# Batch 1 loaded in head halves, h of batches 0 and 1 summed in two steps, and a new order

## The chip, the cores and the metric

The kernel runs on one core of one Trainium2 chip. The metric is device time in microseconds; the time before is 179.36 us, the median of three runs (179.36 to 179.39). A core has engines that run side by side, each through its own list of instructions in order: PE (matrix products, with weight loads shown as PEld), DVE and ACT (elementwise work), POOL and SP (here they mostly issue transfers).

## The reference

```python
kv = einsum('bhsd,bhse->bhde', k, v)            # 8 batches, 8 heads, 576 rows, 64 columns
out = einsum('bhsd,bhde->bhse', q, kv)
x = out / sqrt(mean(out * out, -1) + 1e-6) * g_norm   # heads side by side: 576 x 512
h = maximum(x @ w_in, 0)                        # 512 -> 1024
conv = depthwise convolution of h along the rows, 3 taps, conv_w
y = (h * sigmoid(conv)) @ w_out                 # 1024 -> 512
```

Inputs and outputs are float32; the kernel calculates in bfloat16 with float32 sums.

## The kernel before

Everything is held transposed: columns of x and h lie on the 128 partitions, rows of the sequence along them. Two heads fill 128 partitions, so x of a batch has four blocks (head pairs) t, and h has eight blocks f. A pair of blocks is called u (u = 0 holds t 0 and 1, u = 1 holds t 2 and 3). The 576 rows are cut in two parts s, of 256 and 320 rows for batch 0, 288 and 288 for most others.

A batch goes through these steps, each a small function named by two letters:

- load of q, k and v (`Lq`, `Lk`, `Lv`: transfers on POOL's queue that also turn float32 into bfloat16). Batch 0 comes another way: as float32 by SP's and ACT's queues into staging tiles `stq` and `stg`, then cast on DVE (`cad`) or ACT (`caa`). `gt` makes POOL wait for one of these transfers (k 1) before it issues the weights: `Li` is half of w_in, `Lo` is w_out.
- `kv` (L398) and its copy to SBUF on ACT (`kva`) or DVE (`kvd`); `qt` transposes q (L429), copied by `qa` or `qd`.
- `ot` (L456): q times kv. `sq` (ACT, L505): squares. `on` (PE, L524): sums of squares over a head. `nl` (ACT, L541): reciprocal root, called rs. `mo` (DVE, L552): x. For batches 4 to 7, `oc`, `ss`, `ln`, `sl`, `sp` and `mu` do this for two batches together, and batches 6 and 7 have q transposed by a transfer on SP's queue (`tq`) and use a second copy of kv (`kx`, tile kvx, read by `ox` of s = 1).
- h: `hp` (L643, batch 0), `hs` (L624, batches 1 to 3, 6 and 7) or `hm` (L609, batches 4 and 5) multiply w_in by x: four matmuls, one for each t, are summed in one PSUM bank. `rp` (L650), `rh` (L636) or `re` (L615) apply the Relu on ACT.
- convolution and gate: on DVE in steps `ta`, `aa`, `ab`, with a sigmoid on ACT (`sg`, L683), then the product `mg` (L707); four blocks of batch 0 have the convolution on PE instead (`cv`, L693, with matrices that `dg` builds, and `sc`, L700).
- output: `om` multiplies by w_out (L717) for 128 rows of a pair of batches, `ea` (ACT, L723) or `ed` (DVE, L728) copies the row block, and `st` stores it on SP's queue.
- `fi` multiplies zeros (L282): matmuls whose result nobody uses.

The order is one long string, `ORDER`: tokens like `hp.1.0@0` (f 1, s 0, in PSUM bank 0). The loop at the end of the function calls the steps in that order, and then ties each instruction to the one before it on its engine, so each engine's list is exactly the string's order for that engine. Waits between engines follow from the data and from the buffers, which the number after @ picks. PSUM has eight banks; a bank is free for its next user when its last reader is done. Transfers from POOL carry eight completion counters in turn, and each waits for the one eight before it.

The first tokens of batch 0's h before, and the load of batch 1:

```
mo.0.0.1 fi.1.512@4 on.0.1.1@4 nl.0.1.1@3 mo.0.1.1 Li.0.4 hp.1.0@0 hp.3.0@1 hp.2.0@4 hp.0.0@5 rp.3.0@0 rp.2.0 rp.0.0
pc dg.2 hp.2.1@1 hp.0.1@4 rp.0.1 rp.1.0 hp.1.1@5 Li.4.4 rp.1.1 hp.3.1@2 hp.6.0@0 dg.0 cv.0.0@6 sc.0.0@0 rp.2.1 rp.6.0
```

`Li` and the loads stand here because nothing before them needs them in the string; POOL issues them as soon as its own list gets there.

Of the kernel before, what the change touches and what calls it, by code (L numbers as in the profile page):

```python
# [74 lines left out]
hs.1.5.1@4 ta.1.1.1 aa.1.1.0 ab.1.1.0 hs.1.5.0@5 rh.1.5.0 hs.1.4.1@7 rh.1.4.1 hs.1.4.0@0 rh.1.4.0 rh.1.5.1 hs.1.2.0@1
rh.1.2.0 hs.1.3.0@3 rh.1.3.0 kv.2.0.2@6 sg.0.1.5 mg.0.1.2 ta.1.1.2@1 om.0.3.0.4@3 kva.2.0.2@2 ot.2.1.1@4 ot.2.0.1@0
qt.3.0.0@6 qd.3.0.0@1 om.0.3.4.4 ed.0.3@0 Lk.3.0.4@1 Lv.3.0.4@1 Lq.4.0.4@1 Lk.4.0.4@0 Lv.4.0.4@0 sg.1.1.0 sg.1.1.1
ta.1.1.3 aa.1.1.1 om.0.0.4.4 sq.2.0.1@0 on.2.0.1@6 nl.2.0.1@8 mo.2.0.1@2 sq.2.1.1@1 om.0.1.0.4@3 om.0.1.4.4 ea.0.0@1
on.2.1.1@6 nl.2.1.1@9 mo.2.1.1 ot.2.1.0@0 sq.2.1.0@2 om.0.2.0.4@2 om.0.2.4.4 ed.0.2@2 ea.0.1@3 st.0.0 st.0.1
on.2.1.0@6 nl.2.1.0@0 mo.2.1.0 kv.3.0.2@4 kva.3.0.2@0 ot.2.0.0@2 sq.2.0.0@3 hs.2.0.1@6 mg.1.1.0 rh.2.0.1@1 hs.2.7.1@7  # L80
rh.2.7.1 ta.1.1.5@0 on.2.0.0@4 nl.2.0.0@1 mo.2.0.0 hs.2.3.1@6 rh.2.3.1 hs.1.7.1@7 rh.1.7.1 hs.1.7.0@0 rh.1.7.0
qt.4.1.0@4 qd.4.1.0@2 ot.3.0.1@6 sq.3.0.1@4 qt.3.1.0@2 qd.3.1.0@3 hs.2.3.0@0 rh.2.3.0 ab.1.1.1 on.3.0.1@4 nl.3.0.1@2
mo.3.0.1@0 hs.2.4.1@1 rh.2.4.1 ta.1.1.4 ot.3.1.1@2 sq.3.1.1@5 hs.1.6.0@0 rh.1.6.0 hs.2.4.0@4 rh.2.4.0 ot.3.0.0@6
sq.3.0.0@6 hs.2.2.0@1 rh.2.2.0 on.3.1.1@4 nl.3.1.1@3 hs.2.1.1@0 rh.2.1.1 hs.2.1.0@1 rh.2.1.0 aa.1.1.2 ab.1.1.2
mo.3.1.1 on.3.0.0@4 nl.3.0.0@4 mo.3.0.0 hs.2.2.1@0 rh.2.2.1 ot.3.1.0@2 sq.3.1.0@7 hs.3.1.1@1 rh.3.1.1 hs.3.2.1@0
rh.3.2.1 pl on.3.1.0@4 nl.3.1.0@5 mo.3.1.0 sg.1.1.2 hs.3.3.1@6 Lq.5.0.4@2 Lq.6.0.4@0 Lk.5.0.4@1 hs.3.7.1@7 hs.3.6.1@0
sg.1.1.3 qt.4.0.0@4 qd.4.0.0@0 rh.3.3.1 qt.5.0.0@2 qd.5.0.0@4 hs.3.5.0@1 rh.3.5.0 rh.3.6.1 rh.3.7.1 hs.3.5.1@4
rh.3.5.1 hs.2.0.0@5 hs.3.2.0@2 rh.2.0.0 sg.1.1.5 Lv.5.0.4@1 Lq.7.0.4@1 mg.1.1.1 ta.1.1.6@1 ta.1.1.7 aa.1.1.3
hs.3.0.1@1 rh.3.0.1 hs.3.3.0@0 kv.4.0.2@6 kvd.4.0.2@1 ab.1.1.3 sg.1.1.4 mg.1.1.2 rh.3.3.0 qt.5.1.0@4 qd.5.1.0@1
ta.2.2.3@0 rh.3.2.0 hs.2.6.1@3 rh.2.6.1 sg.1.1.7 sg.1.1.6 mg.1.1.3 hs.3.1.0@1 hs.2.7.0@6 rh.3.1.0 om.0.8.0.4@0  # L90
ot.4.0.0@2 sq.4.0.0@0 rh.2.7.0 ot.4.0.1@4 oc.4.0.1@6 sq.4.0.1@1 om.0.7.0.4@7 hs.3.0.0@1 rh.3.0.0 ta.2.2.2 ta.2.2.1@1
ta.2.2.0 om.0.8.4.4 ea.0.8@4 oc.4.0.0@7 om.0.7.4.4 ed.0.7@5 tq.7.1@3 st.0.7 ot.4.1.0@4 sq.4.1.0@2 oc.4.1.0@8
kv.5.0.2@0 ot.4.1.1@2 oc.4.1.1@9 om.0.4.0.4@6 sq.4.1.1@3 kvd.5.0.2@2 ot.5.0.1@0 aa.2.2.0 aa.2.2.1 ot.5.1.1@4
sq.5.1.1@4 sq.5.0.1@5 oc.5.1.1@0 tq.6.0@0 ab.2.2.0 om.0.4.4.4 ed.0.4@1 oc.5.0.1@1 om.0.5.0.4@7 ot.5.0.0@2 sq.5.0.0@6
ot.5.1.0@4 om.0.5.4.4 Lk.6.0.4@0 Lv.6.0.4@0 ed.0.5@3 hs.3.4.1@0 ab.2.2.1 sq.5.1.0@7 ss.4.4.2@1 ss.5.4.2 ln.4@0 sl.4@0
oc.5.1.0@2 hs.3.7.0@6 rh.3.7.0 om.0.6.0.4@7 rh.3.4.1 oc.5.0.0@3 hs.2.5.0@1 rh.2.5.0 hs.3.6.0@6 rh.3.6.0 kz.6.0.2@4
tq.6.1@2 kvd.6.0.2@0 kx.6@0 sp.4.1.0.4@2 mu.4.1.0@1 sp.4.0.0.4@0 mu.4.0.0 om.0.6.4.4 sg.2.2.1 sp.4.0.1.4@4 mu.4.0.1
sp.4.1.1.4@2 mu.4.1.1 hs.2.5.1@6 rh.2.5.1 ea.0.6@5 st.0.6 hs.3.4.0@0 rh.3.4.0 hs.2.6.0@1 rh.2.6.0 sp.5.0.1.4@4
mu.5.0.1@0 sp.5.1.0.4@6 mu.5.1.0 sg.2.2.0 mg.2.2.0 hm.4.7@2 re.4.7@0 hm.4.5@0 re.4.5 sg.2.2.3 sp.5.1.1.4@4 mu.5.1.1
# [35 lines left out]
def kernel(  # L135
# [511 lines left out]
    @op  # L647
    def rp(f, s):
        r0, r1 = RS[s]
        nc.scalar.activation(  # L650
            h_of(0, f).rearrange("p (e n r) -> p e n r", e=2, r=R)[:, :, :, r0:r1],
            T["hp", f, s].rearrange("p (e r n) -> p e n r", e=2, r=r1 - r0), AX.Relu)
# [157 lines left out]
```

## Time and profile before

| | |
|---|---|
| median of three runs | 179.36 us |
| profiled execution | 179.97 us, of which the span is 178.2 us |
| PE busy | 169.2 us (95%) |
| ACT busy | 150.5 us (84%) |
| DVE busy | 148.4 us (83%) |
| PE fillers (L282) | 40 recorded, 12.7 us |
| transfers of POOL's queue | 14.50 MB |

The span is what the profiler saw between the first and the last instruction; the execution's own time lies 1.77 us above it. Busy time is a union: matmuls overlap one another, so 320 matmuls of 286 ns each can have 43.5 us of busy time. The chain of waits follows the work back from the last instruction to what released it. A row of a timeline gives the start, the busy time, the engine, the line, the tiles and in brackets the idle time in front of it and what ended that.

### The profile page before, as it was taken

What the parts mean: (1) busy time and instruction counts of PE and PEld (TensorE: products, weight loads), DVE (VectorE), ACT (ScalarE), POOL (GpSimd) and SP (SyncE); (2) the same over time, 40 slices, a digit from 0 to 9 for tenths busy, and PEclk for the clock granted to TensorE, in tenths of its full rate; (3) what the DMA queues carried; (4) which work ended last, traced back from release to release, by engine and by line L of the source; (5) the groups of instructions that cost most, each with busy time, mean ns of one, the idle gap of its engine ahead of it and who ended that gap; (6) DMA issues with size and microseconds to landing.
All of it is one profiled execution on the core that took longest, in us unless ns stands there. A gap on an engine that the chain in (4) does not pass through costs nothing.

```text
span 178.2 us, 5048 instructions
## 1 busy us (share of the span) xinstructions
PE 169.2 (95%) x2093; PEld 101.1 (57%) x2109; DVE 148.4 (83%) x285; ACT 150.5 (84%) x273; POOL 20.5 (11%) x32
## 2 busy tenths in 40 slices
...
GB/s 163 392 316 207 208 207 207 209 208 207 207 213 253 208 209 206 181 167 144 174 151 159 135 4 15 180 0 161 109 146 0 0 0 59 123 97 81 318 316 190
DMA packets 25862, 29.10 MB, mean 163 GB/s; under 512 B 5988, under 2 KB 20336, under 8 KB 25840
## 3 DMA queue, kind: packets, MB, share of 16 engines
q0 software_dynamic: 13248, 14.50, 49.0%
...
q8 instruction: 16, 0.26, 0.6%
...
## 4 chain that ended last, share of the span: by engine, by line
PE 78%; ACT 15%; issue 3%; DVE 2%; ACTq 0%
PE banks L717 30%; PE banks L624 15%; PE banks L609 9%; PE banks L282 5%; ACT h L636 4%; PE banks L643 4%; ACT taps L683 3%; ACT sq L505 3%; PE banks L429 2%; PE banks L456 2%; PE banks L398 2%; PE banks L524 2%; PE banks L693 2%; ACT L223 1%; ACT rs L541 1%
## 5 line engine op out<-in xcount | busy, mean ns | idle before, releaser
L717 PE MATMUL banks<-w_out_sb,h 128*128 128x512 bf16 x268 | 63.4, 380 | 0.8 <-issue 0.3
L624 PE MATMUL banks<-x,w_in_sb 128*128 128x288 bf16 (+2 forms) x320 | 43.5, 286 | 1.0 <-issue 0.6
L683 ACT ACTIVATE taps<-taps,cw 128x576 bf16<-128x576 bf16 (+1 forms) x44 | 40.9, 971 | 3.8 <-DVE taps L677 3.8
L717 PEld LDWEIGHTS <-h 128*128 128x128 bf16 x280 | 26.2, 98 | 30.3 <-issue 1.3
L624 PEld LDWEIGHTS <-w_in_sb 128*128 128x128 bf16 x320 | 30.4, 98 | 11.3 <-issue 2.0
L636 ACT ACTIVATE h<-banks 128x288 bf16<-128x288 f32 (+2 forms) x80 | 30.3, 484 | 0.4 <-PE banks L624 0.2
L707 DVE TENSOR_TENSOR h<-h,taps 128x1152 bf16<-128x1152 bf16 (+1 forms) x24 | 22.9, 954 | 6.7 <-ACT h L650 4.1
L505 ACT ACTIVATE sq<-banks 128x576 bf16<-128x576 f32 (+2 forms) x32 | 20.9, 682 | 1.3 <-PE banks L456 1.2
L677 DVE TENSOR_TENSOR taps<-taps,h 128x1152 bf16<-128x1152 bf16 (+1 forms) x22 | 21.4, 973 | 0.5
L672 DVE TENSOR_TENSOR taps<-taps 128x1152 bf16<-128x1152 bf16 (+1 forms) x22 | 21.3, 978 | 0.5
L723 ACT ACTIVATE row<-banks 128x512 f32<-128x512 f32 x25 | 14.8, 603 | 6.0 <-PE banks L717 6.0
L666 DVE TENSOR_SCALAR taps<-h,cw 128x576 bf16<-128x576 bf16 (+1 forms) x44 | 18.5, 421 | 0.3 <-ACT h L650 0.2
L667 DVE TENSOR_SCALAR taps<-h,cw 128x576 bf16<-128x576 bf16 (+1 forms) x44 | 18.5, 421 | 0.0
L552 DVE SCALAR_TENSOR_TENSOR x<-banks,cw,rs 128x576 bf16<-128x576 f32 (+2 forms) x16 | 12.9, 816 | 5.4 <-ACT rs L541 5.3
L609 PE MATMUL banks<-x,w_in_sb 128*128 128x288 bf16 x128 | 16.7, 286 | 0.1
L609 PEld LDWEIGHTS <-w_in_sb 128*128 128x128 bf16 x128 | 12.3, 98 | 4.1 <-issue 0.5
L223 ACT ACT_TABLE_LOAD x10 | 12.8, 1283 | 2.0 <-issue 1.8
L282 PE MATMUL banks<-zero 128*128 128x512 bf16 x40 | 12.7, 450 | 1.4 <-DVE zero L261 1.2
L595 DVE SCALAR_TENSOR_TENSOR x<-o,cw,banks 128x576 bf16<-128x576 f32 (+2 forms) x16 | 12.1, 808 | 0.5 <-PE banks L589 0.5
L541 ACT ACTIVATE rs<-banks,eps_sb 128x576 f32<-128x576 f32 (+2 forms) x16 | 11.6, 738 | 1.1 <-PE banks L524 1.0
L517 ACT ACTIVATE o<-banks 128x576 f32<-128x576 f32 (+2 forms) x16 | 10.5, 683 | 0.5 <-PE banks L496 0.5
L615 ACT ACTIVATE h<-banks 128x576 bf16<-128x576 f32 x16 | 10.0, 673 | 0.5 <-PE banks L609 0.5
...
## 6 DMA issues: line engine op xcount, KB each, us to landing
...
q_sb<-in_q_dram POOLq DMA_DIRECT2D x7, 576.0 KB, 16.4
k_sb<-in_k_dram POOLq DMA_DIRECT2D x7, 576.0 KB, 13.0
v_sb<-in_v_dram POOLq DMA_DIRECT2D x7, 576.0 KB, 15.2
stg<-in_v_dram ACTq DMA_DIRECT2D x2, 576.0 KB, 6.2
...
```

Source lines behind the costliest of these rows:

```text
L282: nc.tensor.matmul(ps[:, :w], zero[:, :P], zero[:, :w], start=True, stop=True)
L505: nc.scalar.activation(T["sq", b, u, s], T["o", b, u, s], AX.Square)
L609: nc.tensor.matmul(ps[:, s, :HS], w_in_sb[:, t, f * P:(f + 1) * P], T["x", b][:, t, c0:c1], start=(t == 0), stop=(t == NT - 1))
L624: nc.tensor.matmul(ps, w_in_sb[:, t, f * P:(f + 1) * P], T["x", b][:, t, c0:c1], start=(t == 0), stop=(t == NT - 1))
L636: nc.scalar.activation(h, fr, AX.Relu)
L666: nc.vector.tensor_scalar_mul(tap[:, 0, f % 2, :n, 8:8 + S], h[:, f], cw[:, f:f + 1])
L667: nc.vector.tensor_scalar_mul(tap[:, 1, f % 2, :n, :S], h[:, f], cw[:, 2 * NF + f:2 * NF + f + 1])
L672: nc.vector.tensor_add(tap[:, 1, :, :n, :S], tap[:, 0, :, :n, 7:7 + S], tap[:, 1, :, :n, 1:1 + S])
L677: nc.vector.tensor_add(y, y, span(b, n)[:, 2 * j:2 * j + 2])
L683: nc.scalar.activation(y, y, AX.Sigmoid, scale=cw[:, NF + f:NF + f + 1])
L707: nc.vector.tensor_mul(h, h, tap_of(b, j)[:, 1, :, :n, :S])
L717: nc.tensor.matmul(T["om", p, m], h[:, f, m * P:(m + 1) * P], w_out_sb[:, f, :], start=(f == 0), stop=(f == NF - 1))
```

## The change

Batch 1's q, k and v, three transfers of four blocks each, become six of two blocks (head pairs u = 0 and u = 1). k and v of u = 0 are issued between the two halves of w_in, the others behind them. A new step `hk` does half of an h group: the matmuls of head pair u alone; its second call closes the sum in the same bank. It takes the place of `hp` (batch 0) and of `hs` for batch 1. All of `ORDER` is new, with other choices of engine for some copies: five casts of batch 0 on ACT in place of two, `kva` five in place of six, `qa` one in place of two, `ea` 23 in place of 25 (with DVE's counterparts the other way), one `oq` (the sum of squares in four small matmuls) in place of one `on`, 39 fillers in place of 44.

```diff
 ORDER = """
-pre@0,1 fi.10.512@0 caa.q.0.0@0 af pn ps cad.v.0.0@0 qt.0.0.0@2 qa.0.0.0@0 fi.8.512@0 ct@0 fi.6.512@1 gt.k.1.0
-caa.v.1.0 cad.k.0.0@0 cad.k.1.0 kv.0.0.1@4 fi.2.512@1 cad.v.2.0 cad.q.1.0 cad.v.3.0 cad.k.2.0 pg cad.k.3.0 cad.q.0.1
...
-qt.0.1.1@0 qd.0.1.1 ot.0.0.1@2 sq.0.0.1@2 ot.0.1.1@6 fi.1.512@0 sq.0.1.1@3 on.0.0.1@0 nl.0.0.1@2 mo.0.1.0 fi.1.512@4
-mo.0.0.1 fi.1.512@4 on.0.1.1@4 nl.0.1.1@3 mo.0.1.1 Li.0.4 hp.1.0@0 hp.3.0@1 hp.2.0@4 hp.0.0@5 rp.3.0@0 rp.2.0 rp.0.0
-pc dg.2 hp.2.1@1 hp.0.1@4 rp.0.1 rp.1.0 hp.1.1@5 Li.4.4 rp.1.1 hp.3.1@2 hp.6.0@0 dg.0 cv.0.0@6 sc.0.0@0 rp.2.1 rp.6.0
-dg.1 cv.0.1@4 sc.0.1 mg.0.1.0 dg.3 hp.4.1@3 rp.4.1 hp.4.0@6 rp.4.0 rp.3.1 hp.5.1@7 rp.5.1 hp.5.0@0 Lq.1.0.4@1
-Lk.1.0.4@1 Lv.1.0.4@1 rp.5.0 hp.7.1@1 rp.7.1 hp.6.1@6 rp.6.1 ta.0.1.5@1 ta.0.1.4 aa.0.1.2 cv.0.2@4 sc.0.2@0 cv.0.3@2
-sc.0.3 qt.1.0.0@0 qd.1.0.0@2 qt.1.1.0@6 qd.1.1.0@3 kv.1.0.1@4 kva.1.0.1@1 kv.1.1.1@2 ot.1.0.1@0 kva.1.1.1 sq.1.0.1@4
-mg.0.1.1 hp.7.0@4 rp.7.0 Lo.0.8 ta.0.1.7@0 ab.0.1.2 ot.1.1.1@2 sq.1.1.1@5 ta.0.1.6 on.1.0.1@6 nl.1.0.1@4 mo.1.0.1@1
-fi.6.512@5 fi.1.512@4 on.1.1.1@4 nl.1.1.1@5 mo.1.1.1 ot.1.0.0@6 sq.1.0.0@6 ot.1.1.0@4 sq.1.1.0@7 on.1.0.0@0 nl.1.0.0@6
-mo.1.0.0 hs.1.3.1@2 rh.1.3.1 aa.0.1.3 ab.0.1.3 hs.1.1.1@3 on.1.1.0@0 rh.1.1.1 nl.1.1.0@7 mo.1.1.0 hs.1.0.1@2 rh.1.0.1
...
+pre@0,1 af pn ps caa.q.0.0@0 cad.v.0.0@0 cad.k.0.0@0 fi.10.512@0 caa.v.3.0 cad.v.1.0 qt.0.0.0@2 fi.10.512@0 qd.0.0.0@0
+ct@0 fi.4.512@1 cad.k.1.0 kv.0.0.1@4 kva.0.0.1@0 cad.v.2.0 fi.4.512@1 caa.q.1.0 pg pc cad.k.3.0 caa.k.2.0 dg.0
+ot.0.0.0@6 sq.0.0.0@0 cad.q.0.1 qt.0.1.0@2 qa.0.1.0@1 fi.3.512@0 oq.0.0.0@4 kv.0.1.1@0 fi.1.512@2 kvd.0.1.1 nl.0.0.0@0
+caa.q.1.1 qt.0.0.1@2 ot.0.1.0@4 sq.0.1.0@1 fi.2.512@0 gt.k.1.0 Li.0.4 Lk.1.0.2@1 Lv.1.0.2@1 Li.4.4 dg.1 qd.0.0.1
+ot.0.0.1@0 sq.0.0.1@2 mo.0.0.0@0 qt.0.1.1@2 qd.0.1.1 on.0.1.0@6 fi.1.512@2 fi.1.512@2 nl.0.1.0@1 mo.0.1.0 on.0.0.1@2
+nl.0.0.1@2 fi.1.512@6 mo.0.0.1 hk.0.0.0.0@6 hk.0.2.0.0@7 ot.0.1.1@4 sq.0.1.1@3 hk.0.0.0.1 rp.0.0@0 fi.2.512@2
+hk.0.2.0.1 rp.2.0 on.0.1.1@2 nl.0.1.1@3 mo.0.1.1 pl hk.0.1.1.0@6 hk.0.2.1.0@0 hk.0.1.0.0@1 hk.0.1.0.1 rp.1.0
+hk.0.3.0.0@7 hk.0.3.0.1 rp.3.0 hk.0.0.1.0@2 hk.0.3.1.0@1 hk.0.0.1.1 rp.0.1 dg.3 hk.0.3.1.1 rp.3.1 hk.0.2.1.1 rp.2.1
+Lq.1.0.2@1 Lq.1.2.2 Lk.1.2.2 Lv.1.2.2 hk.0.1.1.1 rp.1.1 cv.0.0@4 sc.0.0@0 cv.0.3@2 sc.0.3@1 dg.2 cv.0.2@0 cv.0.1@6
+sc.0.1 sc.0.2 kv.1.0.1@4 kvd.1.0.1@1 qt.1.0.0@2 qd.1.0.0@2 hk.0.5.1.0@4 hk.0.5.1.1 rp.5.1 hk.0.5.0.0@5 hk.0.5.0.1
+rp.5.0 ot.1.0.1@6 sq.1.0.1@4 mg.0.1.1 hk.0.4.1.0@4 hk.0.4.1.1 rp.4.1 mg.0.1.0 qt.1.1.0@2 qd.1.1.0@3 hk.0.6.1.0@5
+on.1.0.1@0 hk.0.7.1.0@4 hk.0.6.1.1 kv.1.1.1@2 ta.0.1.5@1 kvd.1.1.1 nl.1.0.1@4 hk.0.7.1.1 rp.7.1 mo.1.0.1@1 ot.1.1.1@2
+sq.1.1.1@5 hk.0.4.0.0@0 rp.6.1 hk.0.6.0.0@1 hk.0.6.0.1 rp.6.0 hk.0.7.0.0@4 on.1.1.1@6 nl.1.1.1@5 hk.1.6.1.0@5
+ta.0.1.6@0 hk.0.7.0.1 rp.7.0 hk.0.4.0.1 rp.4.0 hk.1.1.1.0@1 mo.1.1.1 ot.1.0.0@6 sq.1.0.0@6 hk.1.0.1.0@4 hk.1.2.1.0@0
+hk.1.2.1.1 rh.1.2.1 on.1.0.0@2 nl.1.0.0@6 hk.1.6.1.1 Lo.0.8 Lq.2.0.4@2 Lk.2.0.4@0 Lv.2.0.4@0 Lq.3.0.4@0 hk.1.0.1.1
+hk.1.1.1.1 rh.1.1.1 hk.1.3.1.0@0 ta.0.1.7 rh.1.0.1 aa.0.1.3 ta.0.1.4 Lk.3.0.4@1 Lv.3.0.4@1 hk.1.3.1.1 mo.1.0.0
+ot.1.1.0@2 rh.1.6.1 sq.1.1.0@7 rh.1.3.1 hk.1.5.1.0@1 aa.0.1.2 hk.1.4.1.0@4 hk.1.4.1.1 ab.0.1.3 hk.1.5.1.1 on.1.1.0@6
...
 """
...
     @op
+    def hk(b, f, s, u):
+        c0, c1 = cols(b, s)
+        at = ("hs", b, f, s) if b else ("hp", f, s)
+        if u == 0:
+            T[at] = bank()[:, :c1 - c0]
+        for t in (2 * u, 2 * u + 1):
+            nc.tensor.matmul(
+                T[at], w_in_sb[:, t, f * P:(f + 1) * P], T["x", b][:, t, c0:c1],
+                start=(t == 0), stop=(t == NT - 1))
+
+    @op
     def rp(f, s):
```

The later tokens keep the same steps for batches 2 to 7 in another sequence. Among them, the transposes on SP's queue come in the order `tq.6.0`, `tq.6.1`, `tq.7.0`, `tq.7.1` in place of `tq.7.1`, `tq.6.0`, `tq.6.1`, `tq.7.0`, and the first `ox` is `ox.6.1.1` in place of `ox.6.0.0`.

118 lines of the change are left out of this document (58 added, 60 removed).

## The prediction

> **What bounds the kernel now.** I read the page's head and chain first, then the chain in order of time, then the engines by stretch.
>
> ```profile
> span 178.2 us, 5048 instructions
> ...
> PE 78%; ACT 15%; issue 3%; DVE 2%; ACTq 0%
> ```
> ```profile
> 17.18 4.52 PE banks L643 x36
> ...
> 31.06 1.28 ACT L223
> ...
> 32.36 1.37 ACT rs L541 x2
> ...
> 35.87 0.24 PE banks L524 x2
> 36.12 1.47 PE banks L624 x12
> ```
> ```profile
> core 0: us, PE busy (x) PEld busy (x) DVE busy (x) ACT busy (x) POOL busy (x), PEclk, DMA share, GB/s
> 0.00:17.20 17.20, 14.81 (x204) 6.57 (x208) 10.91 (x44) 8.70 (x15) 8.92 (x17) 1.00 0.97 272
> 17.20:28.80 11.60, 11.60 (x216) 9.26 (x218) 7.19 (x24) 10.04 (x21) 1.09 (x2) 1.00 1.22 208
> 28.80:34.70 5.90, 4.50 (x67) 2.36 (x56) 5.07 (x10) 5.67 (x10) 2.22 (x3) 1.00 1.22 208
> 34.70:112.40 77.70, 76.47 (x1256) 49.04 (x1261) 69.99 (x118) 75.35 (x139) 8.24 (x11) 1.00 1.02 165
> 112.40:142.20 29.80, 29.18 (x222) 17.96 (x217) 27.65 (x38) 28.00 (x50) 0.00 (x0) 1.00 0.24 89
> 142.20:175.10 32.90, 32.64 (x161) 15.95 (x163) 27.55 (x55) 22.38 (x41) 0.00 (x0) 1.00 0.39 146
> ```
>
> PE carries 78% of the chain. From 34.7 to 175.1 us it idles 1.23 + 0.62 + 0.26 = 2.1 us in all, so later stages hold little to win. Two places do: the start, where the first h matmul waits until 17.18 us, and the stretch 28.8 to 34.7 us, where the chain leaves PE for a table load and reciprocal roots of batch 1. ACT is the second full engine: 75.35 of 77.7 us from 34.7 on, 28.00 of 29.8 after that. Work that PE brings forward is kept only if ACT keeps up.
>
> ```profile
> L282 PE MATMUL banks<-zero 128*128 128x512 bf16 x6 | 1.5, 380 | 0.1
> L643 PE MATMUL banks<-x,w_in_sb 128*128 128x256 bf16 x4 | 0.6, 275 | 0.0
> ```
>
> This is PE's list for 28.8 to 34.7 us: 1.5 us of its 4.50 busy are fillers on zeros, and only 0.6 us are h of batch 0. With 5.90 - 4.50 = 1.4 us idle, 2.9 us do nothing.
>
> **The change, part by part.** *Fillers.* 44 become 39. Up to the first h matmul both have 37; before, seven more stand in the gap just described, after, two early in h. They matter only through the gap.
>
> *Start of h.* `hk` splits each group of four matmuls after head pairs 0 and 1, so h can begin when only x of the first pair exists. The number and shapes of its matmuls are the same as of `hp` and `hs`. What it can win at the start is bounded by w_in:
>
> ```profile
> 8.74 1.81 POOL L357 DMA_DIRECT2D w_in_sb<-in_moe_w_in_dram  x2
> 11.28 0.76 POOL L343 DMA_DIRECT2D k_sb<-in_k_dram  x1
> 12.01 0.77 POOL L343 DMA_DIRECT2D v_sb<-in_v_dram  x1
> 16.80 0.74 POOL L343 DMA_DIRECT2D v_sb<-in_v_dram  x1 [1.65 <-ACT sq L505]
> ```
> ```profile
> DMA to landing us min/median/max: 7.5/8.2/8.9
> ```
>
> The last line is w_in's two halves: the first lands at 8.74 + 7.5 = 16.2 us by it, 16.8 at the latest if the issue of v at 16.80, whose code waits for that transfer, names it. Its place in the queue stays. So h starts 0.4 to 1.0 us sooner, at about 16.7.
>
> *Casts moved to ACT.* Five head casts run on ACT instead of two, one `qa` becomes `qd`, one `kva` becomes `kvd`:
>
> ```profile
> 10.13 0.28 ACT L412 ACTIVATE kvb<-banks 128x128 bf16<-128x128 f32 x1 [2.87 <-PE banks L398]
> 10.89 0.60 ACT L505 ACTIVATE sq<-banks 128x512 bf16<-128x512 f32 x1 [0.48 <-PE banks L456]
> 13.38 0.60 ACT L505 ACTIVATE sq<-banks 128x512 bf16<-128x512 f32 x1 [0.48 <-PE banks L456]
> 14.44 0.69 ACT L541 ACTIVATE rs<-banks,eps_sb 128x512 f32<-128x512 f32 x1 [0.47 <-PE banks L524]
> 16.34 1.48 ACT L541 ACTIVATE rs<-banks,eps_sb 128x640 f32<-128x640 f32 x2
> 36.21 0.73 ACT L541 ACTIVATE rs<-banks,eps_sb 128x576 f32<-128x576 f32 x1
> ```
> ```profile
> L382 ACT ACTIVATE v_sb<-stg 128x576 bf16<-128x576 f32 x1 | 0.7, 674 | 0.0
> L382 ACT ACTIVATE q_sb<-stq 128x512 bf16<-128x512 f32 x1 | 0.6, 629 | 1.8 <-DMA stq<-in_q_dram 1.8
> ```
> ```profile
> 8.90 0.46 DVE L380 CAST v_sb<-stg 128x576 bf16<-128x576 f32 x1
> ...
> 17.16 1.68 DVE L552 SCALAR_TENSOR_TENSOR x<-banks,cw,rs 128x640 bf16<-128x640 f32 x2 [1.20 <-ACT rs L541]
> ```
>
> The cast of v block 3 waits on ACT for its transfer, which had landed by 8.90 us; nothing else is ready for ACT until kvb at 10.13, so that one is covered. The other three (q 1.0 0.63, k 2 0.67, q 1.1 about 0.67, together 1.97) stand between kvb and the last rs of batch 0, and so do two Relu (`rp`, about 0.4 each); the second kvb copy (0.28) leaves. That adds 2.5 us to ACT's queue; the idle that it can fill in these rows is 0.48 + 0.48 + 0.47 = 1.43. The last rs of batch 0 ends at 16.34 + 1.48 = 17.82 now; after, from 18.9 (all idle filled) to 20.3 (none). I take 19.4, nearer the first, as one wait stays: `ot.0.1.1` uses banks 4 and 5, which `mo.0.1.0` has to free. Behind it queue on ACT the Relu of f 0 to 3, the table load and the sigmoids; on PE the second halves of h.
>
> PE meanwhile does the first halves. Before, 32 h matmuls are done at 17.18 + 4.52 x 32/36 = 21.2 us; after, about 21.6: x of the second pair follows its rs by one DVE operation (1.68/2 = 0.84), at 20.3, and four matmuls (some 0.13 us each) and small waits follow. So the split alone gains nothing here: 0.4 us behind.
>
> *Batch 1 under h of batch 0.* Before, batch 1's kv, o and norm stand behind nearly all of h of batch 0. After, k and v of its first head half land before w_in's second half, and `kv.1.0.1` stands right behind the four convolutions, with f 4 to 7 left to fill its waits. I laid ACT's and PE's queues out from 19.4 us with these rows:
>
> ```profile
> L650 ACT ACTIVATE h<-banks 128x256 bf16<-128x256 f32 (+1 forms) x16 | 6.0, 487 | 1.2 <-PE banks L643 1.2
> L541 ACT ACTIVATE rs<-banks,eps_sb 128x576 f32<-128x576 f32 (+1 forms) x5 | 3.6, 749 | 0.0
> L700 ACT ACTIVATE taps<-banks,cw 128x576 bf16<-128x576 f32 x4 | 3.0, 740 | 0.1
> ...
> L505 ACT ACTIVATE sq<-banks 128x576 bf16<-128x576 f32 x4 | 2.5, 653 | 0.1
> L636 ACT ACTIVATE h<-banks 128x288 bf16<-128x288 f32 x3 | 1.2, 411 | 0.1
> ```
>
> From the last rs of batch 0 to the last rs of batch 1 (`nl.1.1.0`) ACT has 14 rp (14 x 6.0/16 = 5.25), four sigmoids 3.0, two table loads 2.6 (1.28 each, above), four squares 2.5, four rs (4 x 0.72 = 2.9) and six `rh` (6 x 0.4 = 2.4): 18.65 us, from 19.4 to 38.05, or 38.2 with its small waits. Before it ends at 36.21 + 0.73 = 36.94, but with two `rh` done, not six: the four more are worth 1.6. ACT comes out 1.6 - (38.2 - 36.94) = 0.35 us ahead (0.85 if the rs ends at 18.9, 0.55 behind at 20.3).
>
> PE reaches `on.1.1.0` (now at 35.87) at about 36.75, with 28 matmuls of batch 1's h issued in place of 8. Twenty more at 1.47/12 = 0.122 are 2.45 us, less 0.9 lost: 1.55 ahead. That is the 2.9 us of the gap, less what waits remain and the 0.4 above. So the gain at this point lies between ACT's 0.35 and PE's 1.55; both engines are nearly full behind it, and I take the middle, 0.9.
>
> *Loads.* Three transfers of batch 1 become six; each issue holds POOL about 0.75 us, 2.2 us more, while the queue in front of it is still full: `Lo` (w_out) is issued later, near 16.8, but served in its old place. In bytes the queue's order changes only for w_in's second half, 576 KB later:
>
> ```profile
> k_sb<-in_k_dram POOLq DMA_DIRECT2D x7, 576.0 KB, 13.0
> v_sb<-in_v_dram POOLq DMA_DIRECT2D x7, 576.0 KB, 15.2
> ```
>
> By the medians k and v of batch 1 land at 11.28 + 13.0 = 24.3 and 12.01 + 15.2 = 27.2: 2.9 us for each 576 KB. Then w_in's second half lands at 9.65 + 8.9 + 2.9 = 21.4, needed at about 25.4 when the queues are laid out as above; the last half of v at 27.2, needed at about 28.8. Covered by 4.0 and 1.6 us, if halves run at the rate of wholes; the upper bound of their cost is 3 x 0.75 = 2.2 more, which would show 0.6 us. The Trainium skill, DMA: Bandwidth & Descriptors, section Bandwidth, has a rule against the split: batch transfers to at least 1 MiB, since each has a fixed part. Its fit, about 2.0 us plus the bytes at 436 GB/s per transfer, would put the last half 6 us late by my estimate, were the fixed parts paid in a row, and the sum 4.4 us higher; the 208 GB/s held through 17.2 to 34.7 us speak against that, because queued transfers follow one another without gaps.
>
> *The rest of the order.* Of the later steps, two row copies go from ACT to DVE, two kvb copies to ACT; both kernels load ten tables. These cancel within some tenths on engines that have 9.9 us (DVE) and 4.2 us (ACT) idle from 34.7 to 142.2. On SP the transpose `tq.6.0` now goes first, ahead of rows of pair 0, and `tq.7.1` last, behind `kx.6`:
>
> ```profile
> 77.97 12.04 SPq L463 DMA_TRANSPOSE qT<-q_sb  x2
> DMA to landing us min/median/max: 1.7/3.8/6.6
> ```
>
> Two transposes held SP 12.04 us; the second line is kvx. After, the first `ox` is `ox.6.1.1`, which needs kvx, where before it was `ox.6.0.0`, which does not. By the count of PE's work ahead of them I put kvx's issue near 90 us, which is also when SP came free (77.97 + 12.04), and its use near 96: hidden unless SP is some 3 us later. I cost this part at nothing, with -1 to +2 us as bounds, from the 2.1 us that PE now idles: a new order may close half of it or double it.
>
> **Sum.** 178.2 - 0.9 = 177.3 us of span. The profiled execution took 179.97, 1.77 above its span, and the runs' median, 179.36, is 0.61 below it: 177.3 + 1.77 - 0.61 = 178.5 us.
>
> **Rivals.** *ACT makes it slower.* The three casts hold up batch 0's squares and roots; if its last rs ends past 19.75 us, where ACT's 0.35 is used up, ACT stays behind to the end, as it is full. At 20.3, with one wait of the size seen (0.5) more, it is 1.1 behind: 180.5. For it: ACT's order is fixed and the casts stand first. Against: 1.43 us of idle to fill. Chance 0.23.
> *Hidden.* PE's gain at 35 us returns as waits before 142 us, where ACT is 28.00 of 29.8 busy: 179.0 to 179.7. Chance 0.18.
> *PE sets the pace alone.* 1.55 is kept and half of the 2.1 idle closed: 2.6 less, 176.8 at the most; 177.6 typically. Chance 0.16.
> *A transfer comes late* (the half loads, or kvx behind the transposes at 96 us): PE waits in order, 0.6 to 2.8 us (6.6 - 3.8) on top of the forecast: 179.1 to 181.3. Chance 0.07.
>
> **How the numbers follow.** The forecast, 178.0 to 179.0, has 0.36. Faster by over 0.2%, which is about what a measurement can tell, is forecast and PE alone: 0.52. Same is the hidden case: 0.18. Slower is the rest: 0.30. From 177.2 to 180.6 about 0.2 is left out.
>
> **What would show it.** Right: PE's h of batch 0 starts near 16.7 us; the last rs of batch 0 ends near 19.4; there are no fillers after 20 us and under 1.5 us of PE idle from 21.6 to 35.6; PE is at `on.1.1.0` near 36.75. Wrong: that rs past 20; PE waiting for DMA at kv of batch 1, kz of batch 6 or the first `ox`; or PE idle from 36 to 175 us well over 2.1 us.

## The result and the profile after

The changed kernel takes 181.92 us (median of four runs, 181.82 to 182.34), the kernel before on the same chip 179.38 (179.36 to 179.68): a ratio of 1.0142, interval 1.0123 to 1.0162. The forecast was 178.5 with a range of 177.2 to 180.6, so the time lies outside it. The profiled execution after took 181.96 us with a span of 179.9: 2.06 us lie outside the span, where it was 1.77 before. The profiled execution before took 179.97 us, 0.61 more than its median.

Line numbers: the new `hk` multiplies in L658. What stands behind it is 15 lines lower than before: `ab` L692, `mg` L722, `om` L732, `ea` L738, `ed` L743, `st` L748, `oh` L757, `eh` L767. What stands ahead of it is 4 lines lower (`kv` L402, `kx` L489, `ox` L500, `nl` L545, `hs` L628, `rh` L640).

The page of the changed kernel, its span, the engines and the shares of the chain:

```profile
span 179.9 us, 5061 instructions
...
PE 171.1 (95%) x2106; PEld 99.6 (55%) x2106; DVE 148.7 (83%) x286; ACT 150.3 (84%) x272; POOL 22.4 (12%) x35
...
PE 45%; ACT 24%; DVE 13%; DMA 11%; issue 5%; SPq 1%; POOL 0%; ACTq 0%
```

PE's share of the chain fell from 78% to 45%; ACT, DVE and DMA took it over. Somewhere PE now waits for others. The windows of the changed kernel, with the bounds used before except for the last, which ends with PE's last matmul (columns: busy time and count of PE, PEld, DVE, ACT and POOL, then PEclk, DMA share, GB/s), say where:

```profile
0.00:17.20 17.20, 14.79 (x211) 6.67 (x212) 12.44 (x54) 8.92 (x14) 8.54 (x17) 1.00 0.98 272
17.20:28.80 11.60, 11.52 (x192) 8.28 (x188) 5.62 (x21) 10.89 (x20) 3.26 (x5) 1.00 1.23 206
28.80:34.70 5.90, 5.87 (x83) 3.94 (x82) 4.61 (x12) 5.62 (x13) 2.22 (x3) 1.00 1.23 208
34.70:112.40 77.70, 76.18 (x1242) 46.41 (x1241) 70.24 (x110) 74.20 (x138) 8.40 (x11) 1.00 0.99 174
112.40:142.20 29.80, 29.63 (x230) 18.49 (x230) 28.16 (x39) 28.90 (x51) 0.00 (x0) 1.00 0.20 76
142.20:176.10 33.90, 33.09 (x165) 15.79 (x163) 27.68 (x56) 21.39 (x40) 0.00 (x0) 1.00 0.35 129
```

The gap at 28.8 to 34.7 us is closed: 5.87 of 5.90 us busy, where 4.50 were. In 34.7 to 112.4 PE idles 1.52 us (1.23 before), and in the last window 0.81 (0.26 before). Its list of waits names them:

```profile
PE banks L500 <- DMA kvx<-kvb: 1.3, 1, 1.3
...
PE banks L732 <- ACT row L738: 0.7, 2, 0.5
...
PE banks L658 <- DMA w_in_sb<-in_moe_w_in_dram: 0.5, 1, 0.5
```

Rows of its timeline, in order of time, put them in place (SP's row is the issue of kvx, the copy of kv with its halves swapped that `ox` of s = 1 reads). The second row is batch 0's last root, and the row on DVE shows a wait of that engine for a Relu, which PE's list does not name:

```profile
16.35 0.61 PE L658 MATMUL banks<-x,w_in_sb 128*128 128x256 bf16 x4 [0.49 <-DMA w_in_sb<-in_moe_w_in_dram]
...
18.55 0.78 ACT L545 ACTIVATE rs<-banks,eps_sb 128x640 f32<-128x640 f32 x1
...
91.22 1.18 SPq L489 DMA_DIRECT2D kvx<-kvb  x2
...
96.84 0.30 PE L500 MATMUL banks<-qT,kvx 64*64 64x256 bf16 x4 [1.35 <-DMA kvx<-kvb]
...
147.38 0.76 DVE L692 TENSOR_TENSOR taps<-taps,h 128x1152 bf16<-128x1152 bf16 x1 [1.90 <-ACT h L640]
...
160.59 7.07 PE L732 MATMUL banks<-w_out_sb,h 128*128 128x512 bf16 x32 [0.49 <-ACT row L738]
...
167.90 6.42 PE L732 MATMUL banks<-w_out_sb,h 128*128 128x512 bf16 x28 [0.24 <-ACT row L738]
```

Set against the kernel before, step by step, this gives an account. At `kz.6.0.2` the changed kernel is 1.00 us ahead (84.86 for 85.86). It then waits 1.35 us for kvx, and at `ln.6` it is level (117.69 for 117.78). At `ab.6.1.0` on DVE it falls 1.50 us behind (147.38 for 145.88). DVE's last product ends at 170.64 (169.66 before), PE's last matmul at 176.07 (175.04). From there to the end of the span pass 3.83 us where 3.16 did, and 0.29 more lie outside the span. So by these two traces the lead is lost in one wait, about as much is lost in a second, and the end is longer by nearly a microsecond.

The three add up to 1.99 us between the profiled executions, where the medians differ by 2.54, because the one before was slower than its median. Its timeline has an idle stretch of PE just ahead of `kz.6.0.2` for which the profile shows no cause:

```profile
83.42 0.66 PE L624 MATMUL banks<-x,w_in_sb 128*128 128x288 bf16 x4 [0.63 <-issue]
```

If this stretch is what made that execution slower, which is not shown, the lead against a usual one is up to 0.6 us smaller; the losses behind it stay as they are.

### The profile page after: what moved, and what is told of

Same layout as the page of the kernel before. It is cut to its first block, busy times and chain, and to the rows that moved or that the text cites. A ratio compares the mean times of both kernels' runs of the same rounds, so it can differ in the third digit from the quotient of the medians.

```text
span 179.9 us, 5061 instructions
## 1 busy us (share of the span) xinstructions
PE 171.1 (95%) x2106; PEld 99.6 (55%) x2106; DVE 148.7 (83%) x286; ACT 150.3 (84%) x272; POOL 22.4 (12%) x35
## 4 chain that ended last, share of the span: by engine, by line
PE 45%; ACT 24%; DVE 13%; DMA 11%; issue 5%; SPq 1%; POOL 0%; ACTq 0%
PE banks L732 17%; PE banks L658 8%; ACT h L640 8%; PE banks L628 6%; PE banks L613 6%; ACT taps L698 5%; DMA w_in_sb<-in_moe_w_in_dram 4%; DMA stg<-in_k_dram 4%; DVE h L722 3%; DVE taps L692 3%; DMA kvx<-kvb 3%; ACT o L521 2%; ACT L227 2%; DVE taps L687 2%; DVE taps L682 2%
## 5 line engine op out<-in xcount | busy, mean ns | idle before, releaser
L732 PE MATMUL banks<-w_out_sb,h 128*128 128x512 bf16 x280 | 65.2, 380 | 0.8 <-ACT row L738 0.7
L698 ACT ACTIVATE taps<-taps,cw 128x576 bf16<-128x576 bf16 (+1 forms) x44 | 40.1, 957 | 8.5 <-DVE taps L692 8.4
L732 PEld LDWEIGHTS <-h 128*128 128x128 bf16 x280 | 26.0, 98 | 31.8 <-issue 3.3
L628 PE MATMUL banks<-x,w_in_sb 128*128 128x288 bf16 (+2 forms) x256 | 34.8, 286 | 0.2
L640 ACT ACTIVATE h<-banks 128x288 bf16<-128x288 f32 (+2 forms) x80 | 30.0, 458 | 1.3 <-PE banks L658 0.7
L628 PEld LDWEIGHTS <-w_in_sb 128*128 128x128 bf16 x256 | 24.3, 98 | 8.3 <-issue 1.0
L722 DVE TENSOR_TENSOR h<-h,taps 128x1152 bf16<-128x1152 bf16 (+1 forms) x24 | 22.8, 954 | 3.2 <-ACT taps L698 3.1
L692 DVE TENSOR_TENSOR taps<-taps,h 128x1152 bf16<-128x1152 bf16 (+1 forms) x22 | 21.3, 974 | 2.3 <-ACT h L640 1.9
L658 PE MATMUL banks<-x,w_in_sb 128*128 128x288 bf16 (+2 forms) x128 | 19.2, 287 | 0.5 <-DMA w_in_sb<-in_moe_w_in_dram 0.5
L681 DVE TENSOR_SCALAR taps<-h,cw 128x576 bf16<-128x576 bf16 (+1 forms) x44 | 18.9, 428 | 0.7 <-ACT h L665 0.7
L682 DVE TENSOR_SCALAR taps<-h,cw 128x576 bf16<-128x576 bf16 (+1 forms) x44 | 18.6, 423 | 0.0
L613 PE MATMUL banks<-x,w_in_sb 128*128 128x288 bf16 x128 | 16.7, 286 | 0.1
L738 ACT ACTIVATE row<-banks 128x512 f32<-128x512 f32 x23 | 12.9, 595 | 2.6 <-PE banks L732 2.5
L658 PEld LDWEIGHTS <-w_in_sb 128*128 128x128 bf16 x128 | 11.6, 98 | 5.4 <-DMA w_in_sb<-in_moe_w_in_dram 0.9
L613 PEld LDWEIGHTS <-w_in_sb 128*128 128x128 bf16 x128 | 12.4, 98 | 3.9 <-issue 0.2
L286 PE MATMUL banks<-zero 128*128 128x512 bf16 x39 | 11.6, 427 | 1.3 <-DVE zero L265 1.2
L545 ACT ACTIVATE rs<-banks,eps_sb 128x576 f32<-128x576 f32 (+2 forms) x16 | 11.8, 738 | 1.2 <-PE banks L528 1.0
```

The costliest lines, as they stand in the source:

```text
L613: nc.tensor.matmul(ps[:, s, :HS], w_in_sb[:, t, f * P:(f + 1) * P], T["x", b][:, t, c0:c1], start=(t == 0), stop=(t == NT - 1))
L628: nc.tensor.matmul(ps, w_in_sb[:, t, f * P:(f + 1) * P], T["x", b][:, t, c0:c1], start=(t == 0), stop=(t == NT - 1))
L640: nc.scalar.activation(h, fr, AX.Relu)
L658: nc.tensor.matmul(T[at], w_in_sb[:, t, f * P:(f + 1) * P], T["x", b][:, t, c0:c1], start=(t == 0), stop=(t == NT - 1))
L681: nc.vector.tensor_scalar_mul(tap[:, 0, f % 2, :n, 8:8 + S], h[:, f], cw[:, f:f + 1])
L682: nc.vector.tensor_scalar_mul(tap[:, 1, f % 2, :n, :S], h[:, f], cw[:, 2 * NF + f:2 * NF + f + 1])
```

## The experiments

In the diffs the tokens are those of `ORDER`. Unless said otherwise an experiment starts from the changed kernel. The runs were shared out over chips on which the kernel before took 179.38 to 179.72 us, so a difference between the medians of two runs can be off by 0.3 us; the ratio to the kernel before on the same chip is the surer measure.

**e1: kvx issued earlier.** SP has one list, and `kx.6` stood there behind `st.0.4`, the store of a row block.

```diff
-... ea.0.4@3 sp.5.1.1.4@2 mu.5.1.1@2 sp.5.0.1.4@6 st.0.4 kx.6@0 ...
+... ea.0.4@3 sp.5.1.1.4@2 mu.5.1.1@2 sp.5.0.1.4@6 kx.6@0 st.0.4 ...
```

> The changed kernel with one token moved: kx.6 (the two copies of kv of batch 6 into kvx) stands before st.0.4 on SP's queue, not behind it. Nothing is left out. Theory 'two waits': st.0.4 waits on SP until ACT has copied its row (90.83 us), and kx.6, ready since 86.3, waits behind it; PE then idles 1.35 us before the first ox. Here kvx is issued near 86.5 us, PE's wait before the first ox is gone and ox.6.1.1 starts near 95.5 in place of 96.84; the end comes 0.3 to 1.3 us sooner (181.9 becomes 180.6 to 181.6), less than the wait, because DVE's later wait stays. Rival 'the later part is packed worse as a whole': the wait goes, but PE waits elsewhere before 110 us, the end within 0.3 us of 181.9.

It took 181.49 us, 1.0099 of the kernel before (1.0081 to 1.0118): 0.4 us better than the changed kernel, 0.8 by the ratios. Two rows of its timeline, and the landing times of the tile kvx:

```profile
88.83 1.17 SPq L489 DMA_DIRECT2D kvx<-kvb  x2
...
96.49 0.30 PE L500 MATMUL banks<-qT,kvx 64*64 64x256 bf16 x4 [0.68 <-DMA kvx<-kvb]
...
DMA to landing us min/median/max: 1.9/4.5/7.4
```

The issue came 2.4 us sooner (88.83 for 91.22), not the 4.7 expected, and PE's wait ended only 0.35 sooner (96.49 for 96.84): the transfer itself took longer. A wait of 0.68 stayed. So the place behind `st.0.4` was not the whole reason.

**e2: one Relu earlier.** DVE's `ab.6.1.0` reads f 0 and 1 of batch 6. The tile h holds f, then batch, then row, so f 0 of batch 7 lies inside the stretch from the first to the last element it reads. In ACT's list `rh.7.0.0`, which writes there, stood last of five Relu.

```diff
-... sg.6.1.5 hs.7.5.0@6 hs.7.5.1@7 sg.6.1.4 rh.7.5.1 ... rh.7.1.1 rh.7.5.0 rh.7.6.1 rh.7.0.0 om.2.2.0.4@0 ...
+... rh.7.0.0 sg.6.1.5 hs.7.5.0@6 hs.7.5.1@7 sg.6.1.4 rh.7.5.1 ... rh.7.1.1 rh.7.5.0 rh.7.6.1 om.2.2.0.4@0 ...
```

> The changed kernel with one token moved: rh.7.0.0 (the Relu of f 0, batch 7) stands before sg.6.1.5 on ACT's queue in place of five Relus later. Nothing is left out. Theory 'two waits': DVE's ab.6.1.0 waits from 145.5 to 147.4 us for that Relu, although it reads batch 6 alone, since the two pieces of h lie in one another's range; DVE is the engine that ends last from there on. Here ab.6.1.0 runs near 145.5, the last product mg near 169 in place of 170.6, PE idles under 0.3 us from 142 to 176 us, the end 0.8 to 2.0 us sooner (179.9 to 181.1). Rival 'packed worse as a whole': DVE's wait goes, but the sigmoids or row copies on ACT hold PE as before: within 0.4 us of 181.9.

It took 180.78 us, 1.006 of before (1.0045 to 1.0076): 1.14 us better, 1.5 by the ratios. DVE's row, the same step as at 147.38 above, has no wait any more:

```profile
145.59 0.76 DVE L692 TENSOR_TENSOR taps<-taps,h 128x1152 bf16<-128x1152 bf16 x1
```

Both of PE's waits for row copies (L738) went with it: they were a consequence, since ACT's copies stood behind sigmoids that waited for the late DVE. One token was worth 1.1 to 1.5 us, although DVE is busy 83% of the time. That the wait is one by address range, not by data, is read from the layout; that it hung on this one Relu is shown.

**e3: both.** 

> Both moves of the two kernels before together: kx.6 before st.0.4 and rh.7.0.0 before sg.6.1.5. Nothing is left out. Theory 'two waits': the lead of 1.0 us that the changed kernel has at 85 us reaches the end: 178.3 to 179.2, that is 2.7 to 3.6 us below the changed kernel and below the kernel before. Rival 'packed worse as a whole': the sum of what the two give alone or less, 180.5 or more.

179.99 us, 1.0013 of before (0.9995 to 1.0031): equal to the kernel before, not below it. That is neither the 178.3 to 179.2 of the theory nor the 180.5 or more of its rival. PE's last matmul ends at 174.17 us, 0.9 ahead of before, but kvx still costs 0.8:

```profile
PE banks L500 <- DMA kvx<-kvb: 0.8, 1, 0.8
```

**e4: h in one step.** Each pair of `hk` calls is put together as one `hp` or `hs` at the place of the second call, everything else as in the changed kernel.

```diff
-... hk.0.0.0.0@6 hk.0.2.0.0@7 ot.0.1.1@4 sq.0.1.1@3 hk.0.0.0.1 rp.0.0@0 ...
+... ot.0.1.1@4 sq.0.1.1@3 hp.0.0@6 rp.0.0@0 ...
```

> The changed kernel with each pair of hk calls put together again as one group of four matmuls (hp for batch 0, hs for batch 1), at the place of the second call. Loads and the rest of the order are the changed kernel's. Nothing is left out. Theory 'the split works': the 12 half matmuls done before x of the second pair exists (about 1.5 us) come after it, on.1.1.0 starts 1.0 to 1.5 us later than in the changed kernel (36.24), the end 0.3 to 1.5 us later than 181.9. Rival, as the prediction had it ('the split alone gains nothing at the start'): on.1.1.0 within 0.4 us and the end within 0.3 us of 181.9.

183.51 us, 1.0238 of before (1.0195 to 1.0282). Its windows and the row where PE first stops for x:

```profile
17.20:28.80 11.60, 10.95 (x183) 7.84 (x182) 5.05 (x20) 10.13 (x20) 3.38 (x5) 1.00 1.23 207
28.80:34.70 5.90, 5.29 (x77) 3.46 (x76) 4.59 (x11) 5.65 (x12) 2.23 (x3) 1.00 1.22 207
```
```profile
20.16 2.06 PE L643 MATMUL banks<-x,w_in_sb 128*128 128x320 bf16 x14 [0.49 <-DVE x L552]
```

PE idles 0.65 and 0.61 us where the changed kernel has 0.08 and 0.03, and reaches `on.1.1.0` at 37.68 in place of 36.24. In this order the split is worth 1.4 us there and 1.6 in the time (1.7 by the ratios).

**e5: the transpose behind kvx.** From e3, `tq.7.0`, which stood on SP ahead of `kx.6`, moves behind it. Such a transpose takes 10.3 us from issue to landing by the median of the changed kernel's page.

```diff
-... rh.3.7.0 tq.7.0@4 Lk.6.0.4@0 ... kx.6@0 st.0.4 ...
+... rh.3.7.0 Lk.6.0.4@0 ... kx.6@0 tq.7.0@4 st.0.4 ...
```

> Both moves of e3, and the transpose tq.7.0 behind kx.6 on SP's queue. Theory (kvx is late because it stands behind that transpose in SP's queue): kvx is issued near 84 us and lands before 92, the wait of the first ox (0.8 us in e3) is gone, and the time falls from 179.99 by 0.5 to 0.9 to about 179.2; tq.7.0 is late by some 4 us, but its reader stands near 108 us. Rival (kvx is slow because of the other traffic, or the lead of PE is lost elsewhere): the wait stays at 0.5 or more, or goes and comes back as another, and the time stays at 179.8 to 180.2.

180.00 us, 1.0014 of before (0.9995 to 1.0033): nothing won against e3. Rows of the timeline and the landing times:

```profile
86.41 1.17 SPq L489 DMA_DIRECT2D kvx<-kvb  x2
...
96.02 0.30 PE L500 MATMUL banks<-qT,kvx 64*64 64x256 bf16 x4 [0.47 <-DMA kvx<-kvb]
...
DMA to landing us min/median/max: 1.7/5.2/9.0
```

kvx was issued 4.8 us sooner than in the changed kernel, and PE's wait ended 0.8 sooner. The transpose was not what it waited for.

**e6: the other `ox` first.** From e3. `ox.6.0.0` reads kv itself and not kvx; it goes first, as before, and `ox.6.1.1` comes one `hm` later.

```diff
-... ox.6.1.1@4 sq.6.1.1@0 ta.2.2.4@0 oc.6.1.1@4 ta.2.2.5 ox.6.0.0@2 sq.6.0.0@1 mg.2.2.1 tq.7.1@2 hm.5.4@6 hm.4.0@0 re.5.4 oc.6.0.0@5 ...
+... ox.6.0.0@4 sq.6.0.0@0 ta.2.2.4@0 oc.6.0.0@4 ta.2.2.5 mg.2.2.1 tq.7.1@2 hm.5.4@6 ox.6.1.1@2 sq.6.1.1@1 hm.4.0@0 re.5.4 oc.6.1.1@5 ...
```

> Both moves of e3, and ox.6.0.0 (which does not read kvx) ahead of ox.6.1.1, as in the kernel before; ox.6.1.1 comes behind hm.5.4, some 1.5 us later. Theory (which ox comes first decides whether PE waits): the 0.8 us wait is gone with kvx landing as late as in e3, and the time is 179.1 to 179.4. Rival (the lead of PE is given back by something else, such as ACT's queue): another wait of the same size between 96 and 112 us, 179.8 to 180.2.

179.68 us, 1.0003 of before (0.9992 to 1.0014). PE's rows show both steps without a wait:

```profile
95.44 0.33 PE L500 MATMUL banks<-qT,kvb 64*64 64x320 bf16 x4
...
96.95 0.30 PE L500 MATMUL banks<-qT,kvx 64*64 64x256 bf16 x4
```

The wait is gone and no wait for a transfer or an engine took its place, but only 0.3 of the expected 0.6 to 0.9 us arrived: PE's last matmul ended at 173.77, 1.3 us before that of the kernel before, and the span only 0.6 before. What is left was behind PE.

**e7: the casts back on DVE.** `caa` of v 3, q 1 (both) and k 2 become `cad`; v 3 stands behind v 2 there.

> The changed kernel with the casts of v 3, q 1 (both parts) and k 2 of batch 0 on DVE in place of ACT. Theory (the casts on ACT delay batch 0's roots, as in the prediction's sum): the last rs of batch 0 ends 0.4 to 1.0 us before 19.33, and PE is 0.2 to 0.5 us earlier at 85 us; the time falls by as much, to 181.5 to 181.7, unless the later waits swallow it. Rival (DVE is then the later one, with the building of the matrices for the convolutions between): the rs ends at 19.3 or later and the time is 181.9 to 183.

Its executions scattered between 182.4 and 186.6 us (1.019 of before, 1.0141 to 1.0239), so for the casts only the front of its trace is read. ACT's last root of batch 0:

```profile
19.35 0.78 ACT L545 ACTIVATE rs<-banks,eps_sb 128x640 f32<-128x640 f32 x1
```

It ends at 20.13, 0.8 us later than with the casts on ACT, though four operations left ACT's list: DVE, which also builds the convolution's constants and makes x, was now the later one. The rival was right. For this root ACT was the cheaper place for the casts. The total is no price of the casts alone: in the profiled execution PE waits 2.42 us for kvx, and in the four microseconds from 98 on its granted clock is 0.70, 0.50, 0.50 and 0.59. The ratio is taken from the two executions with a mean clock of 1.00, 182.4 and 183.6 us.

**e8: whole loads.** `Lq`, `Lk` and `Lv` of batch 1 as three transfers behind both halves of w_in.

```diff
-gt.k.1.0 Li.0.4 Lk.1.0.2@1 Lv.1.0.2@1 Li.4.4 ... Lq.1.0.2@1 Lq.1.2.2 Lk.1.2.2 Lv.1.2.2 ...
+gt.k.1.0 Li.0.4 Li.4.4 ... Lq.1.0.4@1 Lk.1.0.4@1 Lv.1.0.4@1 ...
```

> The changed kernel with batch 1 loaded in three whole transfers behind both halves of w_in. Theory (the halves are what lets batch 1 begin under h of batch 0): PE waits about 2.5 us for v at kv.1.0.1, which stood at 24.47 us, as whole v lands near 27.2; the time is 182.8 to 184.2. Rival (the halves are worth nothing, f 4 to 7 and ACT take up the wait): under 0.5 us of wait, 181.5 to 182.3. On the 0.3 us more that lie outside the span: if they come from the three more transfers on POOL's queue, they go back to 1.77 here; if they come from the rest of the order, they stay at about 2.05.

185.54 us, 1.0316 of before (1.0267 to 1.0365): 3.6 us worse than the changed kernel, more than expected. The row of its timeline, and a window behind it:

```profile
27.34 0.48 PE L402 MATMUL banks<-v_sb,k_sb 64*64 64x64 bf16 x36 [2.71 <-DMA v_sb<-in_v_dram]
```
```profile
28.80:34.70 5.90, 5.87 (x103) 3.08 (x102) 3.43 (x8) 4.31 (x8) 0.54 (x1) 0.74 1.22 208
```

The wait is the one that was expected. What comes on top is the clock: PEclk is 0.74 in this window, where the changed kernel has 1.00, and in the four microseconds from 28 on it is 0.71, 0.50, 0.50 and 0.58, which adds up to 1.7 us of full speed lost. The one execution of the four with a mean clock of 1.00 took 184.36 us. By this single one the wait is worth 2.4 us (2.1 by the ratios), and the rest of the 3.6 goes with the slower clock behind it.

The halves are what the new start stands on. They moved the same bytes at the same rate (206 to 208 GB/s in both), so there was no price per transfer to see inside the span. The Trainium skill, DMA: Bandwidth & Descriptors, section Rules for kernel authors, advises to coalesce many small transfers into one large one, and puts the line at 64 KB, under which it is mostly overhead. The halves have 288 KB each. In this queue, which is never empty in that stretch, the run speaks against joining them: what counts is when the first bytes that are needed arrive.

Outside the span e8 has 1.76 to 1.82 us, the changed kernel 2.02 to 2.08.

**e9: the last stores in the order in which their rows are ready.** From e6. The tail of e6 by windows:

```profile
170.00:172.00 2.00, 2.00 (x12) 0.93 (x11) 0.69 (x1) 0.67 (x2) 0.00 (x0) 1.00 1.02 381
172.00:174.00 2.00, 1.77 (x17) 1.35 (x14) 0.69 (x1) 0.52 (x2) 0.00 (x0) 1.00 0.61 220
174.00:176.00 2.00, 0.00 (x0) 0.00 (x0) 0.00 (x0) 0.24 (x1) 0.00 (x0) 1.00 0.88 312
```

The transfer engines are not full at 172 us and are busy with a burst after PE's end. In the kernel before the middle row was full:

```profile
172.00:174.00 2.00, 2.00 (x15) 1.27 (x13) 1.31 (x2) 0.20 (x1) 0.00 (x0) 1.00 0.97 358
```

`st.3.4`, whose row was copied by 171.0 us, stood on SP behind `st.3.7`, whose row came at 171.8.

```diff
-... ed.3.1@0 st.3.1 om.3.0.0.4@4 om.3.0.4.4 ea.3.0@1 om.3.5.0.4@0 st.3.0 ... ea.3.7@3 st.3.7 st.3.4 ...
+... ed.3.1@0 om.3.0.0.4@4 om.3.0.4.4 ea.3.0@1 om.3.5.0.4@0 st.3.0 st.3.1 ... ea.3.7@3 st.3.4 st.3.7 ...
```

> The kernel of e6, and on SP st.3.4 ahead of st.3.7 and st.3.0 ahead of st.3.1, each then in the order in which its row is ready. Theory (the longer end, 3.8 us after PE's last matmul instead of 3.2, is a burst of stores that stood behind a later row while the DMA engines idled at 172 us): st.3.4 goes out some 0.8 us sooner, and the end comes 0.3 to 0.7 us sooner: 179.0 to 179.4, faster than the kernel before by 0.2 to 0.4%. Rival (the end is set by the last half row's own way, whatever stands before it): 179.6 to 179.8.

179.05 us (12 runs), 0.9965 of before (0.9949 to 0.998): below both kernels, by 0.2 to 0.5% below the one before. Its tail:

```profile
172.00:174.00 2.00, 1.86 (x17) 1.42 (x15) 0.69 (x1) 0.44 (x2) 0.00 (x0) 1.00 0.92 340
174.00:176.00 2.00, 0.00 (x0) 0.00 (x0) 0.00 (x0) 0.33 (x1) 0.00 (x0) 1.00 0.60 212
```

Much of what had moved after 174 us now moves before it, and from PE's end to that of the span pass 177.0 - 173.86 = 3.1 us, as in the kernel before.

**e10: q of batch 1 whole, k and v in halves.** From e9.

```diff
-Lq.1.0.2@1 Lq.1.2.2 Lk.1.2.2 Lv.1.2.2
+Lq.1.0.4@1 Lk.1.2.2 Lv.1.2.2
```

> The kernel of e9, with q of batch 1 as one whole transfer where its first half stood (k and v stay in halves). Theory on the time outside the span (each transfer more on POOL's queue costs some 0.09 us there: 0.28 for three): it falls from 2.06 to about 1.96. On the halves: whole q lands some 1.4 us later than its first half did, and k and v of the second half no later; if q's first half had that much to spare, the time falls by 0.1 against e9; if not, it is 0.3 to 1.2 above e9.

179.16 us, 0.9974 of before (0.9959 to 0.9988): the same as e9 within the scatter. q's half is worth nothing; so the loss of e8 belongs to k and v, whose first halves stand ahead of w_in's second half. Outside the span lie 2.14 to 2.23 us, not 1.96 as expected.

**e11: the kernel before, with batch 7's loads in halves.** `Lq.7.0.4`, `Lk.7.0.4` and `Lv.7.0.4` become two transfers each.

> The kernel before, with q, k and v of batch 7 loaded in two halves each, far from the start: three more transfers on POOL's queue and nothing else. Theory (the time outside the span goes by the number of these transfers): 2.05 outside the span in place of 1.77, and a total of 179.7 to 180.3. Rival (it comes from the new order at the start): 1.77.

179.93 us, 1.0014 of before (0.9993 to 1.0035); outside the span 2.12 to 2.23 us in place of 1.70 to 1.84. So halved loads far from the start raise it too.

**e12: the stores behind kvx.** From e5; `st.0.5`, `st.0.8` and `st.0.6`, three row blocks of 256 KB, go behind `kx.6` on SP.

```diff
-... st.0.5 rh.3.7.0 ... kva.6.0.2@0 st.0.8 st.0.6 ab.2.2.1 ... kx.6@0 tq.7.0@4 st.0.4 ...
+... rh.3.7.0 ... kva.6.0.2@0 ab.2.2.1 ... kx.6@0 st.0.5 st.0.8 st.0.6 tq.7.0@4 st.0.4 ...
```

> The kernel of e5 (kx.6 ahead of tq.7.0 on SP) with the three stores st.0.5, st.0.8 and st.0.6 behind kx.6 too. In e5 kvx was issued at 86.4 and landed at 95.5, as late as when it was issued at 88.7 or 91.2. Theory A (kvx waits behind the three stores, 768 KB, in SP's own queue): it lands by 90 us, the wait of the first ox (0.5 us) is gone, and the time is 179.5 to 179.8. Theory B (the DMA engines are full until 96 us, whatever the queue; their share is 1.05 to 1.65 in every 2 us from 78 to 96): kvx still takes 5 us or more and lands past 93; a wait of 0.3 or more stays if it lands past 95.5.

179.34 us, 0.9983 of before (0.9967 to 0.9998), 0.66 better than e5 (0.6 by the ratios; e5's wait was 0.47). Rows of its timeline, and kvx's landing times:

```profile
86.46 1.17 SPq L489 DMA_DIRECT2D kvx<-kvb  x2
87.72 1.50 SPq L748 DMA_DIRECT2D out_dram<-row  x3
...
95.53 0.30 PE L500 MATMUL banks<-qT,kvx 64*64 64x256 bf16 x4
...
DMA to landing us min/median/max: 1.7/3.4/5.0
```

With the same issue time as in e5 the longest landing falls from 9.0 to 5.0 us, and PE does not wait. The transfer engines were about as full: their share from 86 to 88 and from 88 to 90 us is 0.90 and 1.23, in e5 1.12 and 1.13. So the stores ahead in SP's own queue were worth 4 us, and theory A holds for the larger part. The rest, up to 5.0 us for 32 KB beside at best 1.7, remains while the transfer engines are full, as theory B has it: kvx landed near 92, between A's 90 and B's 93. This way out and e9's order of the stores were not run together. The Trainium skill, DMA: Bandwidth & Descriptors, section Queues, rings and completion order, says that each transfer engine consumes one queue's descriptors in order and takes turns between queues. Both parts of what e12 shows agree with it.

## Why the prediction was wrong

- *Start of h* (16.7 us): right, 16.35 with a wait of 0.49 for w_in.
- *Casts moved to ACT* (last root of batch 0 at 19.4, from 18.9 to 20.3): right, 18.55 + 0.78 = 19.33. The rival built on it, ACT that stays behind to the end, did not come about; e7 shows that with these casts on DVE the root comes later still.
- *Batch 1 under h of batch 0* (`on.1.1.0` at 36.75, a gain of 0.9): right, 36.24 and, by the two traces, 1.00 at 85 us. With the later losses mended (e9) the spans, by the medians less the time outside, are 179.05 - 2.09 = 176.96 and 179.56 - 1.77 = 177.79: 0.8 us of the 0.9 reach the end of the span. The forecast's mechanism holds, since the gap at 28.8 to 34.7 us is closed, and so does its size as far as these spans show it, if nothing behind takes it back. What part of the 0.8 the rest of the new order brings is not shown apart.
- *Loads* (covered by 4.0 and 1.6 us): right; PE waits for none of the halves. Without them it waits 2.71 us (e8).
- *"So the split alone gains nothing here"*: this set the first 32 matmuls of h against those of the kernel before and was no measure of the split in the new order, where e4 finds 1.4 to 1.6 us.
- **The step that failed: *The rest of the order*, "I cost this part at nothing, with -1 to +2 us as bounds".** It cost 2.87 us, more than its own upper bound: the difference between the medians of the changed kernel and of e9, in three parts: the Relu that DVE waits for, 1.14 (e2); kvx, 1.10 (e2 to e6); the order of the last stores, 0.63 (e6 to e9). By the ratios to the kernel before the parts are 1.5, 1.0 and 0.7, 3.2 in all. The Relu and the stores were not looked for at all. I had looked at kvx, and had its place right: issue near 90, use near 96, "hidden unless SP is some 3 us later". Measured: issue 91.22, landing 5 us later by the chain below in place of the median 3.8, use at 95.49. The true margin of the forecast was 96 - 93.8 = 2.2 us, not 3, and a median landing was no safe figure for a copy behind row stores in its own queue. A wait of PE for the first `ox` was named as a sign of being wrong. The rival *A transfer comes late* named this wait and a price that holds it, 0.6 to 2.8, and had 0.07; it did not name the other two losses, and its 179.1 to 181.3 ends below the measured time; *Hidden* looked for the loss before 142 us on ACT, where it was a transfer, and most of the rest came after 142.

The two rows of the chain of the changed kernel that carry this:

```profile
91.81 4.99 DMA kvx<-kvb
...
147.38 0.76 DVE taps L692
```

- *Sum*: it took 1.77 us outside the span from the profile before. That was 2.06 after. The 0.3 go with the halved loads: e8, without them, has 1.8, and e11 brings 2.2 into the kernel before by halving loads elsewhere. But it is no price per transfer, since e10, with one transfer less than e9, has 2.19 for 2.09. What it is stays open. With these two terms put right the sum gives 178.5 + 2.87 + 0.29 = 181.7 us for the 181.92 measured; the rest lies within the differences between chips.

One theory of the experiments fell as well: e5 blamed the transpose for kvx's late landing; e12 showed that it was the stores.
